# Scoring the left keys of three head pairs in one block, with their exponentials in two small tiles and the next pair's slot

## The chip, the cores and the metric

One core of one Trainium2 chip runs the whole program. The metric is the time of one execution on the device in microseconds (us); lower is better. Three runs of the kernel before gave 596.84, 598.58 and 599.66 us, a median of 598.58 us.

## The reference

Attention with RMS-normalised queries and keys over 8 batches of 12 heads, 448 tokens and 64 numbers a head, then a two-layer MLP with a residual on the 768 columns of each token.

```python
q_n, k_n = rmsnorm(q, g_q), rmsnorm(k, g_k)          # (8, 12, 448, 64)
scores = q_n @ k_n.T / 8                             # per head, 448 x 448
attn = softmax(scores) @ v
x = attn.transpose(0, 2, 1, 3).reshape(8, 448, 768)
xn = (x - mean(x)) / sqrt(var(x) + 1e-6) * g_ln
out = x + relu(xn @ w_ch1) @ w_ch2                   # 768 -> 3072 -> 768
```

## The kernel before

**Pairs, units, left keys.** The 96 heads are worked on as 48 pairs, p = 0 to 47, six to a batch. From pair 6 on two pairs make a unit, the piece in which q, k and v are loaded and normalised. A pair's keys are 2 heads x 448 tokens: three tiles of 128 keys for each head (i = 0 to 5), and a seventh tile, i = 6, that holds the last 64 keys of both heads. These last 64 are the "left" keys here. A score of i < 6 is one matmul of 128 columns of weights over 448 queries into a bank of PSUM (L388). The left score is two matmuls of 64 columns of weights each, one for a head, that write the lower and the upper 64 partitions of one bank (L394). From unit 5 on (`TWO_LEFT`) both pairs of a unit have their left scores made together, four matmuls in a row, at the first pair's i = 6; the second pair has none at that place.

**Scores, exponentials, values.** `scores` calls `score` (the matmuls) and `power` (L409: ScalarE takes the exponential of the bank into the fp16 tile `E`). `values` multiplies the exponentials by v one pair later (L446 and L448, banks oA and oB), and `evac_o` moves the sums out with VectorE. An even pair's tile has seven slots, an odd pair's six, and the odd pair's left exponentials go to a small tile `EL`.

**Banks.** Score banks are the two `psS` buffers, and, for pairs after 14, the bank `tr` as a third: `score_bank` gives every third score to it. A score waits until the exponential that last read its bank is done: of the score three places before where three banks turn, two places before where two do. The bank `tr` also takes TensorE's transposes of keys and queries (`trans_k`, `trans_q`, copied out by VectorE in `copy_k`, `copy_q`), which pairs up to 13 use. From unit 8 on (pairs 14 and 15) DMA transposes on SP's queue do that: eight for a unit, `dma_k` (L292, L295) and `dma_q` (L302, L305). They write `kU` and `qU`, of which there are two each, so those of a unit wait until the scores of the unit before the last have read the same buffer.

**The order around it.** TensorE, ScalarE, GpSimd and SP run in the order in which the code is written. Up to the middle of pair 12 the table `ORDER` is that order. After it `run_rest` writes the MLP of batch b (24 chunks "up" of six matmuls into psH, each followed by a relu on ScalarE, L1023; then "down" chunks of six into psC, L1055), and after each chunk so many steps of the attention of batch b + 1 as keep pace with it, often one, sometimes two. A step is (p, i); it writes the score of pair p and the values of pair p - 1. The MLP's odd batches have four token tiles (psH 512 wide), the even ones three (384 wide). In `attention()` a unit's preparation is spread over the steps before its first pair p: squares of keys and queries on ScalarE in steps 2 and 4 of pair p - 4, a copy of the keys (L108) in its step 6, roots (L263, L264) in step 1 of pair p - 3, the DMA transposes at the start of pair p - 2. Pairs p - 4 are even ones.

The names that the change touches: `scores`, `score`, `power`, `score_bank`, `copy_q`, `value`, the tiles E7 and E6 (also used as room by the first batch), and the loop in `attention()`.

Of the kernel before, what the change touches and what calls it, by code (L numbers as in the profile page):

```python
# [9 lines left out]
FP16 = mybir.dt.float16  # L10
# [6 lines left out]
ts = bass.ts  # L17

B, H, S, D = 8, 12, 448, 64
# [5 lines left out]
PAIR_UNIT = [(u, w) for u, (_, _, m) in enumerate(UNITS) for w in range(m)]  # L25
UNIT_PAIR = [PAIR_UNIT.index((u, 0)) for u in range(len(UNITS))]
# [38 lines left out]
H0.1.3 Y.R L10v L10q Y.X0 Y.N1 H1.1.0 E12.3 Y.X1 H1.1.1 J0.1 Y.N3 m8 S12.4 Y.X2 H1.1.2 P0.1  # L65
# [55 lines left out]
class _Fast:  # L121


    def __init__(self, ctx, tc, sh, q, k, v, gs, g_ln, w1, w2, out):
        self.gs, self.g_ln = gs, g_ln
        self.tc, self.nc, self.sh = tc, tc.nc, sh
        self.q, self.k, self.v, self.w1, self.w2, self.out = q, k, v, w1, w2, out
        nc = tc.nc
        pool = lambda name, bufs, **kw: ctx.enter_context(tc.tile_pool(name=name, bufs=bufs, **kw))
        self.p_in = pool("p_in", 2)  # L130
        self.p_n = pool("p_n", 2)
        self.p_e = pool("p_e", 1)
# [28 lines left out]
        self.late, self.preps, self.n_scores, self.sums = [], {}, 0, {}  # L161

    def load_main(self, eng, n, t, b, h0, nh):

# [194 lines left out]
    def copy_q(self, p):  # L359
        qT = self.qU[PE_SET][:, p % 2].rearrange("p e s -> p (e s)")  # L360
        self.nc.vector.tensor_copy(out=qT, in_=self.tr[:, 128:128 + 2 * S])  # L361
        kT = self.kT(p)
        self.prs[p] = dict(q=qT, main=kT[:, 192:960], left=kT[:, 0:192])

    def scores(self, p, i):

        u, w = PAIR_UNIT[p]
        both = u >= TWO_LEFT and i == 6
        if both and w:
            return  # L370
        self.score(p, i)
        for d in range(2 if both else 1):
            self.power(p + d, i)

    def score(self, p, i):

        nc = self.nc
        c = self.prs[p]
        both = PAIR_UNIT[p][0] >= TWO_LEFT and i == 6
        if i == 0:  # L380
            k = 7 - p % 2
            c["E"] = self.p_e.tile([128, k, S], FP16, tag=f"E{k}", name="E")
        ps = [self.score_bank(p + d) for d in range(2 if both else 1)]
        for d, x in enumerate(ps):
            self.prs[p + d]["ps", i] = x
        if i < 6:
            h = i // 3
            nc.tensor.matmul(ps[0][:, 0:S], c["main"][:, ts(i, 128)], c["q"][:, ts(h, S)],  # L388
                             start=True, stop=True)
        elif both:  # L390
            for d, x in enumerate(ps):
                cd = self.prs[p + d]
                for e in range(2):
                    nc.tensor.matmul(x[64 * e:64 * e + 64, 0:S], cd["left"][:, 128 * e:128 * e + 64],  # L394
                                     cd["q"][:, ts(e, S)], start=True, stop=True)
        else:
            left, q = c["left"], c["q"]
            nc.tensor.matmul(ps[0][:, 0:S], left[:, 0:128], q[:, 0:S], start=True, stop=False)
            nc.tensor.matmul(ps[0][:, 0:S], left[:, 64:192], q[:, S:2 * S], start=False, stop=True)

    def power(self, p, i):

        c, u = self.prs[p], PAIR_UNIT[p][0]
        if i < 6 or p % 2 == 0:
            o = c["E"][:, i]
        else:
            o = c["EL"] = self.p_e.tile([128, S], FP16, tag="EL", name="EL")
        g = self.group(p, i)
        self.nc.scalar.activation(out=o, in_=c.pop(("ps", i))[:, 0:S], func=AFT.Exp,  # L409
                                  scale=self.units[u][3][:, g:g + 1], bias=EXP_BIAS)  # L410
# [19 lines left out]
    def value(self, p, i):  # L430
        nc = self.nc
        c = self.prs[p]
        E = c["EL"] if i == 6 and p % 2 else c["E"][:, i]
        if i == 0:
            c["oA"] = self.ps_o.tile([128, 3, 130], FP32, tag="oA", name="oA")
            c["oB"] = self.ps_o.tile([128, 130], FP32, tag="oB", name="oB")
        oA, oB = c["oA"], c["oB"]
        if i < 6:
            h, j = divmod(i, 3)
            rhs = self.v16[:, p % 6, h, j]  # L440
            cs = slice(65 * h, 65 * h + 65)
        else:
            rhs = self.vl[:, p % 6].rearrange("p e d -> p (e d)")
            cs = slice(0, 130)
        for t in range(3):
            nc.tensor.matmul(oA[:, t, cs], E[:, ts(t, 128)], rhs,  # L446
                             start=(i == 0 and t == 0), stop=(i == 6 and t == 2))
        nc.tensor.matmul(oB[:, cs], E[:, 320:448], rhs, start=(i == 0), stop=(i == 6))  # L448

# [26 lines left out]
    def first_pieces(self):  # L476
# [9 lines left out]
        E7 = self.p_e.tile([128, 7, S], FP16, tag="E7", name="E").rearrange("p k s -> p (k s)")  # L486
        E6 = self.p_e.tile([128, 6, S], FP16, tag="E6", name="E").rearrange("p k s -> p (k s)")
# [154 lines left out]

        def room(ph, p):
            if ph < 2:
                return (E7 if p < 3 else E6)[:, 896 * (p % 3):896 * (p % 3) + 896]
            return (E6 if p in (2, 3) else E7)[:, 1344 * (p % 2):1344 * (p % 2) + 1344]
# [224 lines left out]
    def attention(self):  # L871
# [25 lines left out]
        for p in range(nb0, n + 1):  # L897
            for i in range(7):
# [1 line left out]
                if i == 0 and p < n and p % NPAIR == 0 and p > nb0:  # L900
                    c.append(lambda b=p // NPAIR: self.batch(b))
                c += todo.pop(7 * p + i, [])
                if p < n and f"S{p}.{i}" not in done and i < 6:
                    c.append(lambda p=p, i=i: self.scores(p, i))
                if p > nb0:
                    for x in {0: (), 1: (0, 1)}.get(i, (i,)):
                        if f"V{p - 1}.{x}" not in done:
                            c.append(lambda p=p, x=x: self.values(p - 1, x))
                if p < n and i == 6 and f"S{p}.6" not in done:
                    c.append(lambda p=p: self.scores(p, 6))  # L910
                if p > nb0 + 1 and i == 1 and (p - 1) % NPAIR and p > 2 * NPAIR:
                    c.append(lambda p=p: self.stats(p - 2))
                if p + 1 < UNIT_PAIR[DMA_UNIT]:
# [419 lines left out]
```

## Time and profile before

| what | us |
|---|---|
| median of three runs | 598.58 (596.84 to 599.66) |
| the profiled execution, its own time | 597.09 |
| its span, first to last instruction | 595.4 |
| VectorE, ScalarE, GpSimd busy | 290.0, 350.9, 191.5 |
| "up" stages of batches 1 to 6 begin at | 112.94, 192.69, 254.28, 330.93, 392.53, 469.18 |
| the "down" stages after them begin at | 154.63, 225.66, 293.80, 363.90, 432.05, 502.15 |
| granted TensorE clock | 0.999 of full speed |

The profile gives the busy time of each engine (PE is TensorE's matmuls, PEld its weight loads, DVE VectorE, ACT ScalarE, POOL GpSimd, SPq the queue that issues DMAs on SP), groups of instructions by line, and for each idle stretch of an engine what ended it. In the timeline a row gives the start and the length of one or several merged instructions. Matmuls overlap: the length of a row is from a matmul's start to the end of its pipeline, and what it costs is the distance to the next one's start.

### The profile page before, as it was taken

The page shows a single profiled execution, that of the slowest core. Times are in us where ns is not written, and L with a number is a line of the kernel's source. Part 1 is how long each engine was busy: PE and PEld are TensorE (multiplying, and loading weights), DVE is VectorE, ACT ScalarE, POOL GpSimd, SP SyncE. Part 2 cuts the span into 40 slices and gives each one's busy share as a digit, 9 for nine tenths or more (in the row PEclk, how much of TensorE's full clock was granted, in tenths as well). Part 3 has the DMA queues.
Part 4 walks back from the last instruction along what each step waited for, and adds up shares of the span by engine and source line. Part 5 has one row for each costly group of instructions (what it writes and reads, how often), then busy time and mean ns, then how long its engine had stood idle before and what let it go on. Part 6 is the DMA issues. An engine that isn't in the chain of part 4 may idle for free.

```text
span 595.4 us, 12406 instructions
## 1 busy us (share of the span) xinstructions
PE 580.2 (97%) x4973; PEld 360.0 (60%) x4973; DVE 290.0 (49%) x634; ACT 350.9 (59%) x664; POOL 191.5 (32%) x256
## 2 busy tenths in 40 slices
PE   5899999999999999999999999999999999999997
PEld 4688986544565666655566666654566666654565
DVE  6999787244455256724356255724256322440011
ACT  6898684279751897358843598538755377114300
POOL 4568550044550555133541345423412000000000
PEclk9999999999999999999999999999999999999999
DMA  8999999725985686945955587849633320040011
GB/s 262 208 243 236 221 233 198 181 72 98 155 157 132 134 152 111 191 117 65 153 139 117 94 138 153 171 122 126 127 66 88 86 63 1 28 106 1 1 53 56
DMA packets 130225, 75.24 MB, mean 126 GB/s; under 512 B 96469, under 2 KB 120357, under 8 KB 130165
## 3 DMA queue, kind: packets, MB, share of 16 engines
q1 hardware_dynamic: 113712, 44.94, 38.3%
q0 software_dynamic: 16128, 29.27, 23.1%
q8 instruction: 40, 0.66, 0.5%
q10 hardware_dynamic: 324, 0.21, 0.1%
q14 instruction: 21, 0.16, 0.1%
HBM read 52.30 MB, written 11.01 MB: 106 GB/s over the span
## 4 chain that ended last, share of the span: by engine, by line
PE 91%; DVE 3%; ACT 2%; DMA 2%; issue 1%; SPq 1%; ACTq 0%
PE psC L1055 36%; PE psH L1021 32%; PE psS L388 8%; PE oA L446 5%; PE psU L718 4%; PE oB L448 2%; PE psS L394 1%; DMA hT<-in_k_dram 1%; SPq L166 1%; PE psS L662 1%; PE tr L339 1%; DMA xnT<-xn 1%; DVE qn L581 0%; ACT khl L116 0%; PE tr L356 0%
## 5 line engine op out<-in xcount | busy, mean ns | idle before, releaser
L1055 PE MATMUL psC<-w,hT 128*128 128x384 f16 (+1 forms) x1368 | 235.5, 323 | 0.0
L1021 PE MATMUL psH<-xnT,w 128*128 128x512 f16 (+1 forms) x1008 | 217.8, 356 | 0.1
L409 ACT ACTIVATE E<-psS,rr_all 128x448 f16<-128x448 f32 x273 | 171.1, 636 | 61.9 <-PE psS L388 61.0
L1055 PEld LDWEIGHTS <-hT 128*128 128x128 f16 x1368 | 127.3, 98 | 78.7 <-issue 3.9
L1023 ACT ACTIVATE hT<-psH 128x512 f16<-128x512 f32 (+1 forms) x168 | 93.7, 558 | 121.4 <-PE psH L1021 120.2
L1021 PEld LDWEIGHTS <-w 128*128 128x128 f16 x1008 | 91.0, 98 | 78.0 <-issue 3.0
L388 PE MATMUL psS<-qU,kU 128*128 128x448 f16 x252 | 86.5, 352 | 0.7 <-ACT E L409 0.6
L446 PEld LDWEIGHTS <-E 128*128 128x128 f16 x819 | 56.1, 98 | 35.3 <-issue 1.4
L268 POOL TENSOR_TENSOR qkv<-qkv,gprod 128x896 f32<-128x896 f32 x20 | 41.6, 2079 | 86.1 <-ACT khl L116 66.0
L1062 DVE SCALAR_TENSOR_TENSOR x<-psC,rs_all,x 128x384 f32<-128x384 f32 x48 | 29.2, 616 | 80.7 <-PE psC L1055 80.2
L446 PE MATMUL oA<-v,E 128*128 128x65 f16 x756 | 58.0, 193 | 0.1
L166 POOL DMA_DIRECT2D qkv<-in_k_dram x14 | 11.2, 797 | 122.8 <-ACT E L409 68.2
L459 DVE RECIPROCAL rec_all<-oA 128x6 f32<-128x6 f32 x42 | 8.2, 195 | 86.4 <-PE oA L446 86.1
L448 PE MATMUL oB<-v,E 128*128 128x65 f16 x252 | 45.2, 193 | 0.1
L260 DVE TENSOR_REDUCE ssq<-khl 128x14 f32<-128x896 f32 x21 | 22.7, 1083 | 45.6 <-ACT khl L116 45.5
L388 PEld LDWEIGHTS <-kU 128*128 128x128 f16 x252 | 24.3, 98 | 16.8 <-DVE qU L361 0.2
L260 DVE TENSOR_REDUCE ssq<-qn 128x14 f32<-128x896 f32 x21 | 22.8, 1085 | 22.2 <-ACT qn L116 21.0
L91 DVE SCALAR_TENSOR_TENSOR qn<-qkv,rr_all 128x256 f16<-128x256 f32 (+2 forms) x71 | 25.3, 416 | 16.9 <-ACT rr_all L264 16.9
L718 PE MATMUL psU<-xnT,w 128*128 128x128 f16 x432 | 26.9, 219 | 0.0
L448 PEld LDWEIGHTS <-E 128*128 128x128 f16 x273 | 26.3, 96 | 0.2 <-DVE xl L466 0.2
L718 PEld LDWEIGHTS <-w 128*128 128x128 f16 x432 | 25.1, 98 | 1.4 <-issue 0.5
L461 DVE TENSOR_TENSOR x<-oA,rec_all 128x384 f32<-128x384 f32 x42 | 23.4, 558 | 1.3
(158 smaller groups left out, 591.9 us busy)
## 6 DMA issues: line engine op xcount, KB each, us to landing
out_dram<-x SPq DMA_DIRECT2D x20, 384.0 KB, 2.6
qkv<-in_v_dram POOLq DMA_DIRECT2D x15, 384.0 KB, 7.3
qkv<-in_k_dram POOLq DMA_DIRECT2D x14, 384.0 KB, 3.8
qkv<-in_q_dram POOLq DMA_DIRECT2D x14, 384.0 KB, 5.3
w<-in_moe_w_ch_dram POOLq DMA_DIRECT2D x3, 1536.0 KB, 12.8
w<-in_moe_w_ch_dram POOLq DMA_DIRECT2D x2, 2304.0 KB, 22.8
qkv<-in_q_dram SPq DMA_DIRECT2D x7, 384.0 KB, 8.8
qkv<-in_v_dram SPq DMA_DIRECT2D x6, 384.0 KB, 13.1
```

The lines of the kernel that those rows point to most:

```text
L91: nc.vector.scalar_tensor_tensor(out=out, in0=x, scalar=8.0, in1=r.unsqueeze(2).broadcast_to([x.shape[0], g, D]), op0=ALU.mult, op1=ALU.mult)
L260: nc.vector.tensor_reduce(out=c["ssq"][:, n], in_=c["sq", n], axis=AX.X, op=ALU.add)
L268: _on(nc, f"i{u}", "P").tensor_tensor(out=self.loads[u][1], in0=self.loads[u][1], in1=sh.gprod.unsqueeze(1).broadcast_to([128, g, D]), op= ...
L388: nc.tensor.matmul(ps[0][:, 0:S], c["main"][:, ts(i, 128)], c["q"][:, ts(h, S)], start=True, stop=True)
L409: self.nc.scalar.activation(out=o, in_=c.pop(("ps", i))[:, 0:S], func=AFT.Exp, scale=self.units[u][3][:, g:g + 1], bias=EXP_BIAS)
L446: nc.tensor.matmul(oA[:, t, cs], E[:, ts(t, 128)], rhs, start=(i == 0 and t == 0), stop=(i == 6 and t == 2))
L448: nc.tensor.matmul(oB[:, cs], E[:, 320:448], rhs, start=(i == 0), stop=(i == 6))
L718: nc.tensor.matmul(ps[:, ts(f, 128)], sh.w1[:, dc, ts(4 * k + f, 128)], self.xnT[:, dc, ts(t, 128)], start=(f == 0 and dc == 0), stop=(f = ...
L1021: nc.tensor.matmul(ps[:, 0:N], sh.w1[:, dc, ts(f, 128)], xnT[:, dc, 0:N], start=(dc == 0), stop=(dc == NDC - 1))
L1023: nc.scalar.activation(out=hT[:, f, 0:N], in_=ps[:, 0:N], func=AFT.Relu)
L1055: nc.tensor.matmul(self.psC[:, 0:g[1]], self.hT[:, f, ts(t, 128)], sh.w2[:, h, f, c:c + g[1]], start=(f == 0), stop=(f == NFF - 1))
L1062: self.nc.vector.scalar_tensor_tensor(out=x, in0=self.sums.pop((b, t, g[0]))[:, 0:g[1]], scalar=self.rs[:, b, t:t + 1], in1=x, op0=ALU.mul ...
```

## The change

From pair 12 on the left scores of three pairs 3m, 3m + 1 and 3m + 2 are made in one block of six matmuls. In a batch's six pairs the two blocks stand in pair 1 after its score 3 (with scores 4 and 5 behind it, one step later than before), and in pair 3 at its place 6. Pairs 0, 2 and 5 have no left score at their place 6, and pair 4's score 5 comes one step later. All pairs' tiles have six slots now. The exponentials of pair 3m's left keys go to slot 5 of the next pair's tile, which that pair fills later; the other two go to two `EL` buffers. Pair 13's TensorE transposes and copies (K13, C13, Q13, D13) stand in the table, and the bank `tr` is a third score bank as soon as the last of them is written.

```diff
-Y.X3 H1.1.3 J1.1 H2.1.0 H2.1.1 J2.0 S12.5 P1.1 P2.0 y8 H2.1.2 H2.1.3 E12.5 J2.1 P2.1 E12.4 M
+H0.1.3 Y.R L10v L10q Y.X0 Y.N1 H1.1.0 E12.3 Y.X1 H1.1.1 J0.1 Y.N3 m8 S12.4 K13 C13 Y.X2 H1.1.2
+P0.1 Y.X3 H1.1.3 J1.1 H2.1.0 H2.1.1 J2.0 S12.5 Q13 D13 P1.1 P2.0 y8 H2.1.2 H2.1.3 E12.5 J2.1
+P2.1 E12.4 M
...
+THREE_LEFT = 12
...
     def copy_q(self, p):
...
+        self.all_turned = p + 1 == UNIT_PAIR[DMA_UNIT]
...
     def scores(self, p, i):
-        u, w = PAIR_UNIT[p]
-        both = u >= TWO_LEFT and i == 6
-        if both and w:
+        if i == 6:
+            self.left_scores(self.left_pairs(p))
             return
         self.score(p, i)
-        for d in range(2 if both else 1):
-            self.power(p + d, i)
+        self.power(p, i)
+
+    def score_at(self, p, i):
+        if p < THREE_LEFT or p % 6 == 3:
+            return i
+        return {1: (0, 1, 2, 3, 6, 4, 5), 4: (0, 1, 2, 3, 4, None, 5)}.get(
+            p % 6, (0, 1, 2, 3, 4, 5, None))[i]
+
+    def left_pairs(self, p):
+        if p >= THREE_LEFT:
+            return range(p - p % 3, p - p % 3 + 3)
+        if PAIR_UNIT[p][0] >= TWO_LEFT:
+            return () if PAIR_UNIT[p][1] else (p, p + 1)
+        return (p,)
+
+    def left_scores(self, pairs):
+        for x in pairs:
+            self.left_score(x)
+        for x in pairs:
+            self.power(x, 6)
...
+    def open_powers(self, p):
+        c = self.prs[p]
+        if "E" not in c:
+            c["E"] = self.p_e.tile([128, 6, S], FP16, tag=f"E{p % 2}", name="E")
+
+    def left_score(self, p):
         nc = self.nc
         c = self.prs[p]
-        both = PAIR_UNIT[p][0] >= TWO_LEFT and i == 6
...
+        for e in range(2):
+            nc.tensor.matmul(ps[64 * e:64 * e + 64, 0:S], left[:, 128 * e:128 * e + 64],
+                             q[:, ts(e, S)], start=True, stop=True)
...
     def power(self, p, i):
         c, u = self.prs[p], PAIR_UNIT[p][0]
-        if i < 6 or p % 2 == 0:
             o = c["E"][:, i]
+        elif p >= THREE_LEFT and p % 3 == 0:
+            self.open_powers(p + 1)
+            o = c["EL"] = self.prs[p + 1]["E"][:, 5]
         else:
-            o = c["EL"] = self.p_e.tile([128, S], FP16, tag="EL", name="EL")
+            o = c["EL"] = self.p_e.tile([128, S], FP16, tag="EL", name="EL", bufs=2)
...
     def score_bank(self, p):
         self.n_scores += 1
-        if p > UNIT_PAIR[DMA_UNIT] and self.n_scores % 3 == 2:
+        if self.all_turned and self.n_scores % 3 == 2:
...
-                if p < n and f"S{p}.{i}" not in done and i < 6:
-                    c.append(lambda p=p, i=i: self.scores(p, i))
+                at = self.score_at(p, i)
+                score = lambda p=p, at=at: self.scores(p, at)
+                go = p < n and at is not None and f"S{p}.{at}" not in done
+                if go and i < 6:
+                    c.append(score)
...
-                if p < n and i == 6 and f"S{p}.6" not in done:
-                    c.append(lambda p=p: self.scores(p, 6))
+                if go and i == 6:
+                    c.append(score)
```

How the instructions move is seen in three places. The first is TensorE in the first "up" stage of the attention of batch 2, at the left scores of pair 14 (before, with pair 15) and of pairs 15, 16 and 17 (after). The rows are from the program before. In a row, the line comes first, then the operation, the tile written and the tiles read; psS is a score bank, kU0 or kU1 the unit's turned keys; a row that stands for the second head's matmul reads like the first and is left out.

```order
L448 MATMUL oB_2509<-vl_109,EL_2359 128x130
L394 LDWEIGHTS kU0_104
L394 MATMUL psS_2598<-qU0_106,kU0_104 64x448
...
L394 MATMUL psS_2599<-qU0_106,kU0_104 64x448
L1021 LDWEIGHTS w1_68
L1021 MATMUL psH_2608<-xnT_2191,w1_68 128x512
```

The same place in the changed program, three pairs of it, and what follows.

```order
L475 MATMUL oB_2626<-vl_109,EL_2432 128x130
L422 LDWEIGHTS kU0_104
L422 MATMUL psS_2714<-qU0_106,kU0_104 64x448
...
L422 LDWEIGHTS kU1_105
L422 MATMUL psS3_2717<-qU1_107,kU1_105 64x448
...
L422 MATMUL psS_2720<-qU1_107,kU1_105 64x448
L404 LDWEIGHTS kU1_105
L404 MATMUL psS_2743<-qU1_107,kU1_105 128x448
L1051 LDWEIGHTS w1_68
L1051 MATMUL psH_2746<-xnT_2194,w1_68 128x512
```

The block takes all three banks (psS3 is `tr`), reads two units' keys, and here has pair 16's first score behind it with no MLP chunk between. Of the twelve blocks one is followed by a score at once, three by four value matmuls and then a score, the other eight by a chunk of the MLP before the next score.

The second place is ScalarE beside these blocks; before, then after. L1023 (L1053 after the change) is the relu of a chunk, L409 (L436) the exponential, L108 the copy of a unit's keys.

```order
L409 ACTIVATE E_2488<-psS_2574,rr_all_1828 128x448
L1023 ACTIVATE hT_120<-psH_2581 128x512
L108 ACTIVATE khl_2531<-qkv_2063 128x14x64
L409 ACTIVATE E_2488<-psS_2598,rr_all_1828 128x448
L409 ACTIVATE EL_2606<-psS_2599,rr_all_1828 128x448
L1023 ACTIVATE hT_120<-psH_2608 128x512
```

```order
L436 ACTIVATE E_2607<-psS_2689,rr_all_1830 128x448
L1053 ACTIVATE hT_120<-psH_2696 128x512
L436 ACTIVATE E_2723<-psS_2714,rr_all_1830 128x448
L436 ACTIVATE EL_2725<-psS3_2717,rr_all_2331 128x448
L436 ACTIVATE EL_2728<-psS_2720,rr_all_2331 128x448
L436 ACTIVATE E_2723<-psS_2743,rr_all_2331 128x448
L1053 ACTIVATE hT_120<-psH_2746 128x512
```

The block has left the even pair's place 6, where the copy of the keys stands ahead of its exponentials; it has three exponentials in a row, the first into the tile (E_2723) that the next score's exponential writes too.

The third place is TensorE at pair 13's transposes into `tr`, at the end of the table. Before, keys and queries followed each other within the "up" stage of batch 1:

```order
L1021 MATMUL psH_2302<-xnT_2191,w1_68 128x512
L336 LDWEIGHTS khl_1525
L336 MATMUL tr_121<-id16_58,khl_1525 128x2x64
...
L339 MATMUL tr_121<-id16_58,khl_1525 128x128
L353 LDWEIGHTS qn_1524
L353 MATMUL tr_121<-id16_58,qn_1524 128x2x64
...
L1021 MATMUL psH_2326<-xnT_2191,w1_68 128x512
```

After the change the keys' stand behind pair 12's score 4 and the queries' behind its score 5, in the "down" stage of batch 0:

```order
L404 MATMUL psS_2217<-qU1_107,kU1_105 128x448
L339 LDWEIGHTS khl_1526
L339 MATMUL tr_121<-id16_58,khl_1526 128x2x64
...
L1085 MATMUL psC_2198<-w2_62,hT_120 128x384
...
L404 MATMUL psS_2257<-qU1_107,kU1_105 128x448
L356 LDWEIGHTS qn_1525
L356 MATMUL tr_121<-id16_58,qn_1525 128x2x64
...
L1085 MATMUL psC_2243<-w2_62,hT_120 128x384
```

24 matmuls of the MLP now lie between the keys' transposes and the queries'.

More of the change, by code (lines that the diff above doesn't have):

```diff
@@ L161, in __init__ @@
         self.late, self.preps, self.n_scores, self.sums = [], {}, 0, {}
+        self.all_turned = False
     def load_main(self, eng, n, t, b, h0, nh):
@@ new lines, in left_pairs @@
+    def left_pairs(self, p):
[9 more added lines that the diff above has]
+            self.power(x, 6)
+    def score(self, p, i):
+        if i == 6:
+            for x in self.left_pairs(p):
+                self.left_score(x)
+            return
+        c = self.prs[p]
+        if i == 0:
+            self.open_powers(p)
+        c["ps", i] = ps = self.score_bank(p)
+        self.nc.tensor.matmul(ps[:, 0:S], c["main"][:, ts(i, 128)], c["q"][:, ts(i // 3, S)],
+                              start=True, stop=True)
@@ L377, in score @@
+    def open_powers(self, p):
+        c = self.prs[p]
+        if "E" not in c:
+            c["E"] = self.p_e.tile([128, 6, S], FP16, tag=f"E{p % 2}", name="E")
+    def left_score(self, p):
         nc = self.nc
         c = self.prs[p]
-        both = PAIR_UNIT[p][0] >= TWO_LEFT and i == 6
[L380 to L399, printed above, removed]
+        c["ps", 6] = ps = self.score_bank(p)
@@ L401, in power @@
+        left, q = c["left"], c["q"]
+        if PAIR_UNIT[p][0] < TWO_LEFT:
+            nc.tensor.matmul(ps[:, 0:S], left[:, 0:128], q[:, 0:S], start=True, stop=False)
+            nc.tensor.matmul(ps[:, 0:S], left[:, 64:192], q[:, S:2 * S], start=False, stop=True)
+            return
+        for e in range(2):
+            nc.tensor.matmul(ps[64 * e:64 * e + 64, 0:S], left[:, 128 * e:128 * e + 64],
+                             q[:, ts(e, S)], start=True, stop=True)
     def power(self, p, i):
@@ L432, in value @@
         c = self.prs[p]
-        E = c["EL"] if i == 6 and p % 2 else c["E"][:, i]
+        E = c["EL"] if i == 6 else c["E"][:, i]
         if i == 0:
@@ L485, in first_pieces @@
         wide = [x.rearrange("p w e s -> p (w e s)") for x in self.qU]
[L486 to L487 removed]
+        Ea = self.p_e.tile([128, 6, S], FP16, tag="E0", name="E").rearrange("p k s -> p (k s)")
+        Eb = self.p_e.tile([128, 6, S], FP16, tag="E1", name="E").rearrange("p k s -> p (k s)")
         self.batch(0)
@@ L644, in room @@
             if ph < 2:
-                return (E7 if p < 3 else E6)[:, 896 * (p % 3):896 * (p % 3) + 896]
-            return (E6 if p in (2, 3) else E7)[:, 1344 * (p % 2):1344 * (p % 2) + 1344]
+                return (Ea if p < 3 else Eb)[:, 896 * (p % 3):896 * (p % 3) + 896]
+            return (Eb if p in (2, 3) else Ea)[:, 1344 * (p % 2):1344 * (p % 2) + 1344]
         PARTS = {2: (((0, 0, 192), (1, 0, 192), (2, 0, 128)), ((2, 128, 192), (3, 0, 192), (4, 0, 192)),
```

2 lines of the change are left out of this document (1 added, 1 removed).

## The prediction, on record before the run

> **What bounds the kernel now.** I read the page first, then the stages, the waits, and the timeline around one block. From the page of the profile:
>
> ```profile
> span 595.4 us, 12406 instructions
> ...
> PE 580.2 (97%) x4973; PEld 360.0 (60%) x4973; DVE 290.0 (49%) x634; ACT 350.9 (59%) x664; POOL 191.5 (32%) x256
> ...
> PE 91%; DVE 3%; ACT 2%; DMA 2%; issue 1%; SPq 1%; ACTq 0%
> ```
>
> TensorE is busy 97% of the span and 91% of the chain that ended last, so a change pays here only by matmul time saved or by idle time of TensorE; all of that is 595.4 - 580.2 = 15.2 us. The view by stretches, for the "up" stages of batches 1, 2 and 4 (span, then the busy time of each engine, then the granted clock and the share of the DMA engines):
>
> ```profile
> 113.00:154.00 41.00, 39.93 (x269) 19.75 (x270) 16.64 (x38) 30.64 (x56) 18.77 (x26) 1.00 0.48 104
> 192.70:225.70 33.00, 33.00 (x290) 20.57 (x289) 14.91 (x37) 28.87 (x60) 18.52 (x26) 1.00 0.76 138
> 330.90:363.90 33.00, 33.00 (x290) 20.54 (x288) 14.87 (x37) 28.83 (x60) 18.42 (x26) 1.00 0.86 136
> ```
>
> TensorE is full there at the full clock, but ScalarE has 28.8 of 33 us to do, so a burst on it finds little slack. The waits of TensorE from 112 us on, and where the left scores are seen as a group:
>
> ```profile
> PE tr L353 <- DVE kU L346: 0.8, 1, 0.8
> PE psS L388 <- ACT E L409: 0.6, 3, 0.2
> ...
> L394 PE MATMUL psS<-qU,kU x80: 352/365/377, 71.4 to 501.9; 128*64 128x448 f16 x80
> ```
>
> So where the change works (all of the 80/4 = 20 blocks of left scores but the first two, which the table holds) TensorE loses 1.4 us in waits. Nothing of 3 us (0.5%, about what a measurement of this kernel can tell from no change) can be gained there beyond the matmuls' own cost.
>
> **The blocks: 18 of two pairs become 12 of three.** One block of two, in time order, and the same values followed by a chunk without a block (338.82, 338.87); the row at 347.12 is the second pair's two matmuls, from a view that cuts into the block:
>
> ```profile
> 338.82 0.22 PE L448 MATMUL oB<-vl,E 128*128 128x130 f16 x1
> 338.87 1.14 PE L1021 MATMUL psH<-xnT,w 128*128 128x384 f16 x6
> ...
> 346.59 0.33 PE L446 MATMUL oA<-vl,EL 128*128 128x130 f16 x3
> 346.76 0.22 PE L448 MATMUL oB<-vl,EL 128*128 128x130 f16 x1
> 346.91 0.57 PE L394 MATMUL psS<-qU,kU 128*64 128x448 f16 x4
> ...
> 347.12 0.35 PE L394 MATMUL psS<-qU,kU 128*64 128x448 f16 x2
> ...
> 347.41 1.15 PE L1021 MATMUL psH<-xnT,w 128*128 128x384 f16 x6
> ```
>
> From the value matmul to the chunk it is 0.65 us with the block and 0.05 without: a block of two costs 0.60. Its pairs start 0.21 apart, less than half of that, so 0.60 - 2 x 0.21 = 0.18 is paid for going in and out. A block of three then costs 0.81, and six pairs 2 x 0.81 = 1.62 instead of 3 x 0.60 = 1.80. Six batches: **-1.1 us**. Bounds: if the third pair cost as much as half a block (0.30), nothing; if it started as close as an ordinary score's 0.19, -1.3. I take the row's 0.21.
>
> [...]
>
> **Pair 13's transposes.** They move from the "up" stage into the "down" stage before it. Their matmuls cost the same there; the wait between them does not move along. The first two rows are from the new place, pair 12's score 4 and the 24 matmuls behind it, the others from the old one:
>
> ```profile
> 106.49 0.35 PE L388 MATMUL psS<-qU,kU 128*128 128x448 f16 x1
> 106.68 4.06 PE L1055 MATMUL psC<-w,hT 128*128 128x384 f16 x24
> ...
> 118.72 0.66 DVE L346 COPY kU<-tr 128x960 f16<-128x960 f16 x1 [4.87 <-PE tr L339]
> 119.43 0.22 PE L353 MATMUL tr<-id,qn 128*128 128x128 f16 x1 [0.75 <-DVE kU L346]
> ```
>
> The queries' transposes waited 0.75 us for VectorE's 0.66 us copy out of `tr`. At the new place 4.06 us of matmuls cover that copy, six times its length; without that cover the 0.75 would be back. **-0.75 us**, bounds -0.75 and 0.
>
> **Waits for a bank that go.** Three scores waited for an exponential:
>
> ```profile
> 124.65 0.35 PE L388 MATMUL psS<-qU,kU 128*128 128x448 f16 x1 [0.18 <-ACT E L409]
> ...
> 227.18 0.35 PE L388 MATMUL psS<-qU,kU 128*128 128x448 f16 x1 [0.19 <-ACT E L409]
> ...
> 365.43 0.35 PE L388 MATMUL psS<-qU,kU 128*128 128x448 f16 x1 [0.18 <-ACT E L409]
> ```
>
> The first is pair 13's, with two banks in turn; it now has three. The other two are the second of two scores behind a block whose exponentials stood behind the copy of the keys; the block has left that place. **-0.55 us**; at least nothing, at most the 0.6 of the list.
>
> **Waits for a bank that come.** A block of three takes every bank. The next score needs the bank of the block's first pair, and the block's third pair the bank of the score just before the block. What ScalarE does around the block above:
>
> ```profile
> 346.61 0.51 ACT L1023 ACTIVATE hT<-psH 128x384 f16<-128x384 f32 x1
> ...
> 346.98 0.67 ACT L409 ACTIVATE E<-psS,rr_all 128x448 f16<-128x448 f32 x1
> ...
> 347.50 0.53 ACT L1023 ACTIVATE hT<-psH 128x384 f16<-128x384 f32 x1
> 347.87 1.00 ACT L108 ACTIVATE khl<-qkv 128x896 f16<-128x896 f32 x1
> 348.39 0.35 PE L388 MATMUL psS<-qU,kU 128*128 128x448 f16 x1
> ...
> 348.71 0.68 ACT L409 ACTIVATE E<-psS,rr_all 128x448 f16<-128x448 f32 x1
> 349.22 0.69 ACT L409 ACTIVATE EL<-psS,rr_all 128x448 f16<-128x448 f32 x1
> ```
>
> An exponential holds ScalarE 0.51 (348.71 to 349.22) and is done after 0.68; a relu of 384 holds it 0.37 and starts 0.02 after its chunk. In the new places (odd pairs, places 4 and 6) there is no copy of keys. With the block's start as zero, its first pair ends at 0.38 (0.57 less 0.21, and a little), the last chunk's relu is over by then, so the first exponential runs from about 0.4 to 1.05. A score directly behind the block would start at 0.29 + 2 x 0.21 = 0.72 and waits about 0.35 (one place); with four value matmuls between, which are half as wide as the four from 346.59 to 346.81 and so take some 0.13, it waits 0.2 (three places); with a chunk of 1 us between, not at all (eight). The third pair starts at 0.43: where a chunk lies between it and the score before, that score's exponential is long done; only the last batch's second block has none between, up to 0.3. Sum 0.35 + 3 x 0.2 + 0.2 = 1.15; an exponential late by half its length at these places (ScalarE is 87% busy) adds some. **+1.4 us**, bounds 0.6 and 2.5 (0.5 each at five places). Queued behind a late score are only the next chunk's matmuls, so the loss is the wait itself.
>
> **Transposes that are needed earlier.** The block in pair 3 reads pair 4's and 5's keys and queries, and pair 1's last score, which frees their buffer, comes a step later. Where slack is least, unit 18 (pairs 34, 35):
>
> ```profile
> 337.36 0.35 PE L388 MATMUL psS<-qU,kU 128*128 128x448 f16 x1
> ...
> 337.75 2.27 SPq L292 DMA_TRANSPOSE kU<-khl  x1
> 340.07 5.37 SPq L295 DMA_TRANSPOSE kU<-khl  x2
> ...
> 349.44 3.56 SPq L305 DMA_TRANSPOSE qU<-qn  x2
> ...
> DMA to landing us min/median/max: 4.2/4.2/4.2
> ...
> 355.31 0.22 PE L448 MATMUL oB<-vl,E 128*128 128x130 f16 x1
> ```
>
> They start when pair 31's score 5 (337.36) ends. Of the last two the first landed 4.2 after its start, at 353.6 (the row of landings, from the view of L305); the second was issued at 353.0, and for its landing I take 354.1, an estimate. Now pair 31's score 5 stands a chunk and some values later, by about 2.3 us, so the last lands at about 356.4, and the block stands behind the values at 355.31, say at 355.9 with the other shifts, its second pair at 356.1. They meet within 0.3 us. For unit 12, in a batch of the same kind, the same sum leaves 2 us:
>
> ```profile
> 199.50 2.48 SPq L292 DMA_TRANSPOSE kU<-khl  x1
> ...
> 208.58 3.72 SPq L305 DMA_TRANSPOSE qU<-qn  x2
> ...
> 216.90 0.33 PE L446 MATMUL oA<-vl,E 128*128 128x130 f16 x3
> ```
>
> (issued by 212.3, landed by 213.4, + 2.3 = 215.7, needed at about 217.7.) Batches with 512-wide chunks have longer steps and more slack. **+0.3 us**, bounds 0 and 4.3 (rival B). The block in pair 1 reads pair 2's transposes, which start with pair 0; pair 0's steps run ahead of the last 13 chunks (of 1 us each) of the batch before, so these have time.
>
> **Semaphores inside a block.** The first reader of a unit's transposes has extra wait instructions:
>
> ```profile
> L388 PEldq EVENT_SEMAPHORE  x32: 51/51/51, 130.9 to 492.7; - x32
> ```
>
> Before they stood ahead of a 128-wide score under a running chunk. Ten or so units are now first read inside a block, between short matmuls. Two of 51 ns for each of 12 blocks would be 1.2 us; hidden, nothing. **+0.3 us**.
>
> Sum: -1.1 - 0.75 - 0.55 + 1.4 + 0.3 + 0.3 = **-0.4 us**. The profiled execution took 597.09, so it would take 596.7 with a span of 595.0; the median of the runs is 1.49 higher, and against it the forecast is **598.1 us**.
>
> **The rivals.** *A: none of the new waits binds.* The exponential of the block's first pair is always in time, the transposes too, and the semaphores are hidden: the +2.0 goes, -2.4 is left, 596.2 us. For it speaks that ScalarE's heavy pieces stand in even pairs, and the blocks now in odd ones; against it the arithmetic at the score directly behind a block.
>
> *B: the transposes come late.* The place is the second pair of the block in pair 3 of batches 3, 5 and 7, and it decides once eight transposes take over 16 us from pair 1's last score. Unit 18 took 15.3 us to issue, with 5.4 for its two L295 while the DMA engines were 0.86 busy; unit 12 took 12.8. With another 3 us of such sticking in the two batches that still load, unit 18 is late by 3.3 and unit 12 by 1: +4.3 instead of +0.3, 602.1 us. Against it: in the list above TensorE waits for no DMA at all.
>
> *C: ScalarE falls behind in every block.* Three exponentials in a row hold it 1.5 us, and relus behind them free psH late. If each of the 12 blocks cost TensorE 0.5, the +1.4 becomes 6.0: 602.7 us. It decides from a backlog over one chunk; against it, 4 us of slack in each 33.
>
> *D: a third pair drains like a block of its own.* Nothing is saved on the blocks: +0.7 in sum, 599.3 us.
>
> **How the numbers follow.** The forecast 0.47, A 0.18, B 0.12, C 0.11, D 0.12. The forecast's own range is 596.5 to 600, which covers A and D nearly; B and C, 0.23 together, reach over 601.6, so the upper end must go to 601.7 to leave out no more than about half of them, and the lower to 595.5 for A with a run-to-run spread like the one shown (596.84 to 599.66). Faster by over 0.5% (under 595.6) 0.13: A at its bounds. Slower by over 0.5% (over 601.6) 0.19: B and most of C. Same 0.68.
>
> **What would show it.** After the change the left matmuls start in threes 0.21 apart, 14 blocks in all; no wait of queries' transposes at 119 us; waits of scores for exponentials of 0.2 to 0.4 at four or five places, all right behind blocks. A wait for a DMA on a left score, above all near 356 us, would be B; waits of psH for relus C. I am wrong if TensorE's idle time after 113 us grows or shrinks by over 2 us.

## The result, and the profile after

The changed kernel took 595.89 us (median of 10 runs, 594.75 to 598.48) against 598.66 before (10 runs, 596.84 to 599.66): a ratio of 0.9962, 95% interval 0.9949 to 0.9975, so 0.38% faster. The forecast was 598.1, faster by 0.1%.

The profiled execution happens to be the slowest of its ten. Its page and its list of TensorE's waits from 40 us on (what waited for what: total, times, longest):

```profile
span 596.8 us, 12425 instructions
...
PE 578.8 (97%) x4973; PEld 360.6 (60%) x4973; DVE 289.0 (48%) x634; ACT 352.0 (59%) x664; POOL 192.9 (32%) x256
...
PE psS L404 <- ACT EL L436: 2.2, 2, 2.0
...
PE psS L404 <- ACT E L436: 1.0, 4, 0.4
```

The span is longer than before's 595.4, although TensorE is busy 1.4 us less. The wait of 2.0 us stands in the table's part, and neither of the two other profiles of the same kernel has it:

```profile
93.42 0.35 PE L404 MATMUL psS<-qU,kU 128*128 128x448 f16 x1 [2.01 <-ACT EL L436]
```

So total spans of single executions can't be compared here: the part ahead of the first "up" chunk of batch 1, where the loads of the first inputs run, differs by up to 3 us from one execution of this kernel to another. The stretch from that chunk to the end is steady, and the readings below rest on it. The second profile of the changed kernel, page and the row of the chunk:

```profile
span 593.9 us, 12425 instructions
...
PE 579.4 (98%) x4973; PEld 361.7 (61%) x4973; DVE 289.2 (49%) x634; ACT 351.6 (59%) x664; POOL 193.5 (33%) x256
```

```profile
113.93 1.24 PE L1051 MATMUL psH<-xnT,w 128*128 128x512 f16 x5
```

593.9 - 113.9 = 479.9; in the three profiles of the changed kernel it is 479.93, 479.92 and 480.16, in two of the kernel before 482.50 and 482.73. Of these 2.6 us, 0.8 is work that moved ahead of the stretch (pair 13's transposes), as this view of the second profile shows at their new place:

```profile
106.92 0.35 PE L404 MATMUL psS<-qU,kU 128*128 128x448 f16 x1
107.11 0.22 PE L339 MATMUL tr<-id,khl 128*128 128x128 f16 x1
107.17 0.50 PE L342 MATMUL tr<-id,khl 128*128 128x128 f16 x6
107.50 4.06 PE L1085 MATMUL psC<-w,hT 128*128 128x384 f16 x24
```

Seven transposes cost 107.50 - 107.11 = 0.39 us, the two sets 0.78; no wait is left. So the change gains 1.8 us in the stretch.

A block of three, from the timeline of the second profile, whole and then cut after its second and its first pair:

```profile
354.10 0.22 PE L475 MATMUL oB<-vl,EL 128*128 128x130 f16 x1
354.25 0.76 PE L422 MATMUL psS<-qU,kU 128*64 128x448 f16 x6
354.94 0.50 PE L1051 MATMUL psH<-xnT,w 128*128 128x384 f16 x2
```

```profile
354.25 0.57 PE L422 MATMUL psS<-qU,kU 128*64 128x448 f16 x4
```

```profile
354.25 0.38 PE L422 MATMUL psS<-qU,kU 128*64 128x448 f16 x2
```

From the value matmul to the chunk it is 0.84 us, 0.05 of it without a block: a block of three costs 0.79 where a block of two cost 0.60. Two blocks of three in place of three blocks of two save 1.80 - 1.58 = 0.22 in each batch, 1.3 in six. The third pair adds 0.19, as an ordinary score does, not 0.21; the starts in the trace are 0, 213 and 403 ns.

A score behind a block with four value matmuls between, in the second profile (TensorE, then ScalarE):

```profile
197.61 0.76 PE L422 MATMUL psS<-qU,kU 128*64 128x448 f16 x6
198.30 0.27 PE L473 MATMUL oA<-v,E 128*128 128x65 f16 x3
198.41 0.19 PE L475 MATMUL oB<-v,E 128*128 128x65 f16 x1
198.78 0.35 PE L404 MATMUL psS<-qU,kU 128*128 128x448 f16 x1 [0.19 <-ACT E L436]
...
199.06 0.19 PE L475 MATMUL oB<-v,E 128*128 128x65 f16 x1
199.09 0.32 PE L1051 MATMUL psH<-xnT,w 128*128 128x384 f16 x1
```

```profile
197.72 0.49 ACT L1053 ACTIVATE hT<-psH 128x384 f16<-128x384 f32 x1 [0.27 <-PE psH L1051]
198.11 0.63 ACT L436 ACTIVATE E<-psS,rr_all 128x448 f16<-128x448 f32 x1
198.62 1.16 ACT L436 ACTIVATE EL<-psS,rr_all 128x448 f16<-128x448 f32 x2
```

The first exponential runs from 0.50 to 1.13 us after the block's start and the score begins 0.04 later. The idle time in the score's brackets is 0.19, but the instruction behind that value matmul normally starts 0.03 later (199.06, 199.09) and here starts 0.37 later: the score lost 0.34, because idle time is counted only from the modelled end of the matmul before (198.41 + 0.19 = 198.60). Read so, from start to start against the same pair of instructions elsewhere in the trace, the five waits behind and in blocks cost 0.46, 0.44, 0.35, 0.35 and 0.24, together 1.84 us.

### The profile page after: what moved, and what is told of

The parts are those of the page before. It is cut to its first block, busy times and chain, and to the rows that moved or that the text cites. A ratio compares the mean times of both kernels' runs of the same rounds, so it can differ in the third digit from the quotient of the medians.

```text
span 596.8 us, 12425 instructions
## 1 busy us (share of the span) xinstructions
PE 578.8 (97%) x4973; PEld 360.6 (60%) x4973; DVE 289.0 (48%) x634; ACT 352.0 (59%) x664; POOL 192.9 (32%) x256
## 4 chain that ended last, share of the span: by engine, by line
PE 82%; DMA 9%; SPq 3%; POOL 2%; ACT 1%; issue 1%; DVE 1%; POOLq 0%; DVEq 0%
PE psC L1085 36%; PE psH L1051 33%; PE psS L404 7%; PE oA L473 4%; DMA qkv<-in_v_dram 4%; DMA qkv<-in_k_dram 2%; DMA qkv<-in_q_dram 2%; SPq L169 2%; PE oB L475 2%; SPq L177 1%; PE psS L422 1%; DMA w<-in_k_dram 1%; ACT E L436 0%; ACT hT L1053 0%; POOL qkv L271 0%
## 5 line engine op out<-in xcount | busy, mean ns | idle before, releaser
L436 ACT ACTIVATE E<-psS,rr_all 128x448 f16<-128x448 f32 x264 | 165.1, 635 | 62.6 <-PE psS L404 62.3
L1053 ACT ACTIVATE hT<-psH 128x512 f16<-128x512 f32 (+1 forms) x168 | 93.6, 557 | 110.5 <-PE psH L1051 108.9
L473 PEld LDWEIGHTS <-E 128*128 128x128 f16 x792 | 53.7, 98 | 35.4 <-issue 3.1
L475 PEld LDWEIGHTS <-E 128*128 128x128 f16 x264 | 25.4, 96 | 0.3 <-DVE xl L493 0.2
```

Of the source, the lines that this page charges most:

```text
L473: nc.tensor.matmul(oA[:, t, cs], E[:, ts(t, 128)], rhs, start=(i == 0 and t == 0), stop=(i == 6 and t == 2))
L1053: nc.scalar.activation(out=hT[:, f, 0:N], in_=ps[:, 0:N], func=AFT.Relu)
```

## The experiments

The stretch from the first "up" chunk of batch 1 to the end, in each profile. The third column adds 0.8 where pair 13's transposes stand ahead of the stretch, so that it can be compared down the column.

| kernel | stretch, us | same work | median, runs | ratio to before |
|---|---|---|---|---|
| before (two profiles) | 482.50, 482.73 | 482.6 | | 0.9989 (0.9975 to 1.0004) |
| changed (three profiles) | 479.93, 479.92, 480.16 | 480.8 | 595.89, 595.67, 595.93 | 0.9962, 0.9958, 0.9955 |
| e1 list only | 480.28 | 481.1 | 596.09 | 0.9962 (0.9948 to 0.9977) |
| e2 blocks only | 480.95 | 480.9 | 596.66 | 0.9972 (0.9958 to 0.9986) |
| e4 chunk apart (two profiles) | 478.17, 478.33 | 479.0 | 594.34, 594.41 | 0.9929, 0.9925 |
| e5 blocks of one | 482.88 | 483.7 | one run | |
| e7 tiles only | 481.69 | 481.7 | 596.98 | 0.9979 (0.9967 to 0.9991) |
| e8 transposes late | 490.16 | 491.0 | one run | |
| e9, e10 twice | 499.18, 503.21 | 500.0, 503.2 | one run each | |

**One part alone.** e1 has blocks of two, e2 the old place of pair 13's transposes, e7 both, so only the tiles and the earlier third bank are left in it. The table's rows are cut to the entries that differ.

```diff
-THREE_LEFT = 12            # e1, e7
+THREE_LEFT = 99
-m8 S12.4 K13 C13 Y.X2      # e2, e7
+m8 S12.4 Y.X2
-J2.0 S12.5 Q13 D13 P1.1
+J2.0 S12.5 P1.1
```

> The changed kernel with blocks of two as before (the bound from which three pairs are scored together set past the last pair); kept are pair 13's transposes in the table, the third bank from pair 13 on, tiles of six slots and two small tiles. Theory (the gain is the sum of the parts seen after 113 us in the two traces): the 0.75 us wait of the queries' transposes goes and the first waits for a bank shrink, so 0.8 to 1.2 us faster than before, about 0.15 to 0.2%. Rival (the gain comes from the tiles and the order in the table, ahead of 113 us): 2 us or more faster, as much as the whole change.

> The changed kernel with pair 13's transposes back in the steps of pair 12, behind the table; blocks of three stay. Theory: blocks of three at 0.79 instead of 0.81 us save 1.3 us, new waits behind blocks cost about as much as the old bank waits that go, and the 0.75 us wait between keys' and queries' transposes is back: 0.8 to 1.5 us faster than before, 0.15 to 0.25%. Rival (the parts need each other: the third bank comes too late for the first block): no gain, and a wait of over 0.5 us at the first block.

> The changed kernel with blocks of two and pair 13's transposes back in the steps of pair 12: what is left of the change is the tiles (six slots for all, two small ones), and the third bank from the end of pair 13's transposes on. Theory (the list's transposes are what the kernel with blocks of two gains by): within 0.15% of before, about 0.5 us faster by the earlier third bank, and the 0.75 us wait between the transposes is back. Rival (the tiles give the early part more room): 1.5 us or more faster, nearly as much as with the transposes in the table.

In the stretch, e7 gains 0.8 to 0.9 over before, e1 1.5, e2 1.7, the change 1.8. e7's share is larger than the expected 0.5: the three waits for a bank that the earlier third bank removes (before at 124.65, 128.35 and 138.81 us) lose 0.34, 0.17 and 0.29 us from start to start, 0.8 together, of which the list of idle times shows only the first. The last of them in the kernel before:

```profile
138.49 0.19 PE L448 MATMUL oB<-v,E 128*128 128x65 f16 x1
138.81 0.35 PE L388 MATMUL psS<-qU,kU 128*128 128x448 f16 x1
```

Putting the transposes into the table adds 0.6 to that (e7 to e1). Blocks of three add 0.3 on top (e1 to the change), since most of what the matmuls save goes to the new waits. e2 stands only 0.1 behind the change: it pays 0.9 more for the transposes at their old place, but it has four waits in and behind blocks (0.34, 0.35, 0.35 and 0.23) where the change has five, 0.6 less. Its profile also has waits of 0.9 for a copy and 0.7 for a DMA, both ahead of the stretch.

By medians the parts look larger: e1 is 1.85 us under the kernel before and e7 1.55, above what both expectations said, and for e7 within its rival's "1.5 us or more", a gain in the early part. The traces don't bear that rival out: e7's first "up" chunk came at 112.83 us, hardly earlier than before's 112.94 and 113.31, and the kernel before, run again beside e7 (e6 below), stood 0.9 under the same reference runs. The intervals, 0.3% wide, can't separate the parts.

**The change and the kernel before, again.**

> The changed kernel as it is, beside the others on the same chip. Theory: the parts add, 1.6 to 2.5 us faster than before. Its second profile should show no 2 us wait near 93 us if that wait was a chance of one execution, and the same wait if the two small tiles cause it.

> The kernel before, as it is. It shows how far the stretch ahead of the first up chunk (112.94 us in its first profile; 113.9 to 117.8 in the changed kernel and the three others) varies between executions, and that the stretch after it does not. Theory: 482.5 us again from the first up chunk to the end, within 0.5, and a first up chunk somewhere between 113 and 117. Rival: the changed kernel is quicker ahead of that chunk, and 112.94 was a lucky execution: 115 or later here.

> The changed kernel as it is, a third time. Theory: 479.9 us from the first up chunk to the end, and 1.6 to 2.3 us under the kernel before.

The stretches repeat within 0.25 us. By medians the change is 2.3 us faster than before in e3, as expected, and 2.8 in e12, more than the 1.6 to 2.3 expected there. The first "up" chunk came at 116.91, 113.93 and 114.38 us in the changed kernel and at 112.94 and 113.31 before; with 0.8 of moved work in the former no gain ahead of it is seen. The 2 us wait at 93 us did not come back: it was a chance of one execution. The kernel before, submitted beside its own reference runs, came out at 597.65 against 598.53, ratio 0.9989, with an interval that takes in 1. So some of the 2.3 to 2.8 us in the comparisons of medians may not be the change's; against that 597.65, which was not run beside them, the change's medians are 1.7 to 2.0 lower, as the stretch says. Where the remaining 0.5 to 1 us lies is open.

**A chunk on both sides of every block (e4, e11).** A step that holds a block is written alone.

```diff
+        self.blocks = set()
...
+                if go and at == 6:
+                    self.blocks.add(len(steps))
                 if c:
                     steps.append(c)
...
     def upto(self, target):
+        ran = False
         while self.pos < min(target, len(self.steps)):
+            block = self.pos in self.blocks
+            if block and ran:
+                break
             for call in self.steps[self.pos]:
                 call()
             self.pos += 1
+            ran = True
+            if block:
+                break
```

> The changed kernel, with one rule more where steps are written behind the MLP's chunks: a step that holds a block is written alone, so a chunk stands between the score before it, the block, and the score behind it. Theory (a score behind a block waits for the block's first exponential only because no chunk is between): the waits of 0.2 to 0.4 us behind four blocks and inside the last block go, 1.3 us of idle time, 1.2 to 1.8 us faster than the changed kernel. Rival (ScalarE's backlog sets them): the waits move to the next scores, less than 0.5 us gained.

> The kernel with a chunk on both sides of every block, again, beside the changed kernel on the same chip. Theory: from the first up chunk to the end 478.2 us again, and 1.7 us under the changed kernel's median. Rival (its first comparison was helped by the chip): less than 0.8 us under it.

478.2 and 478.3 instead of 479.9: 1.7 us, the 1.84 of the five waits nearly whole. The ratio to before is 0.9929 (0.9913 to 0.9945) and 0.9925 (0.9909 to 0.9941), and beside the changed kernel the median is 1.3 and 1.5 us lower. From 100 us on TensorE's list of waits is empty. The place of the wait above, in e4's timeline:

```profile
197.72 0.76 PE L423 MATMUL psS<-qU,kU 128*64 128x448 f16 x6
198.41 0.27 PE L474 MATMUL oA<-v,E 128*128 128x65 f16 x3
198.52 0.19 PE L476 MATMUL oB<-v,E 128*128 128x65 f16 x1
198.54 1.14 PE L1054 MATMUL psH<-xnT,w 128*128 128x384 f16 x6
199.52 0.35 PE L405 MATMUL psS<-qU,kU 128*128 128x448 f16 x1
```

The chunk starts 0.02 after the value matmul, and the score, 1.80 after the block's start, finds its bank free. So the waits came from the lack of a chunk, not from ScalarE's backlog: they did not move to the next scores. In both comparisons this version is ahead of the changed kernel too, by 0.2% of its time.

**What a block pays for being one (e5).** Every pair's left score stands alone at its own place 6.

```diff
     def score_at(self, p, i):
-        if p < THREE_LEFT or p % 6 == 3:
-            return i
+        return i
...
         if p >= THREE_LEFT:
-            return range(p - p % 3, p - p % 3 + 3)
+            return (p,)
...
-        elif p >= THREE_LEFT and p % 3 == 0:
-            self.open_powers(p + 1)
-            o = c["EL"] = self.prs[p + 1]["E"][:, 5]
```

> The changed kernel with each pair's left score alone at its own place 6 from pair 12 on: 36 blocks of one instead of 12 of three. Theory (each block pays once for going into and out of the half-width matmuls, about 0.18 to 0.2 us, and 0.2 a pair): a block of one costs 0.39 us, 36 of them 14.0 us against 9.5 for 12 of three, so 4 us and a little more in the stretch from the first up chunk to the end (479.9 in the changed kernel, then 483 to 485; less the bank waits of about 1.3 that go). Rival D (each pair drains for itself, nothing hangs on the number of blocks): the stretch shrinks by the bank waits alone, to 478.5.

A block of one in its timeline:

```profile
307.20 0.22 PE L471 MATMUL oB<-vl,EL 128*128 128x130 f16 x1
307.35 0.38 PE L421 MATMUL psS<-qU,kU 128*64 128x448 f16 x2
307.66 1.15 PE L1081 MATMUL psC<-w,hT 128*128 128x384 f16 x6
```

It costs 0.46 - 0.05 = 0.41, so 36 of them 14.8 us against 9.5 for 12 of three: 5.3 more, less the 1.84 of waits that it doesn't have, 3.4. Measured 483.7 - 480.8 = 2.9, in one execution, and 482.88 is just under the expected 483 to 485; the other 0.5 is not explained. Rival D (478.5) is out: one, two and three pairs cost 0.41, 0.60 and 0.79, that is 0.22 a block and 0.19 a pair.

**Transposes late.** e8 moves the DMA transposes of units 9 to 24 four steps later in the written order; e9 (the changed kernel) and e10 (the one before) issue the key transposes of units 12, 18 and 24 twice.

```diff
-                at = st + (e - st) * x // (k - 1) if x < k else e + 1 + x - k
+                at = st + (e - st) * x // (k - 1) if x < k else e + 1 + x - k + (4 if u > DMA_UNIT else 0)
```

```diff
         def dma_k():
+            for _ in range(2 if u in (12, 18, 24) else 1):
+                keys()
+
+        def keys():
```

> The changed kernel with the DMA transposes of all units after the first (units 9 to 24) issued four steps later, some 5 us. It measures the margin of rival B. By the landing times in the changed kernel's trace, 2.5 to 3.5 us are left at units 12, 18 and 24: late by about 2 us in each of three batches, 4 to 8 us more in the stretch from the first up chunk, with TensorE waiting for transposes at the block in pair 3. If nothing is lost, the margin is wider than the landings say.

It lost 10.2 us, more than the expected 4 to 8, and not at a block. Unit 12's transposes started at 200.59 us as before (200.68): on SP's queue nothing that waits longer came ahead of them (the issue before them, at 192.16, was over by 193.27), and they start when the scores that free their buffer are done: in the first profile of the changed kernel the transposes of each of units 9 to 24 start 0.03 to 0.04 us after a score ends, unit 12's at 203.66 after one that ends at 203.63. The loss is at the "up" stages of batches 3 and 5. TensorE's waits, and its row at the first of them:

```profile
PE psH L1051 <- DMA xnT<-xn: 6.9, 2, 3.6
...
256.14 2.72 PE L1051 MATMUL psH<-xnT,w 128*128 128x512 f16 x6 [3.29 <-DMA xnT<-xn]
```

SP's queue there in e8, and in the second profile of the changed kernel:

```profile
246.65 2.51 SPq L308 DMA_TRANSPOSE qU<-qn  x2
249.26 5.23 SPq L1033 DMA_TRANSPOSE xnT<-xn  x4
```

```profile
241.56 2.53 SPq L308 DMA_TRANSPOSE qU<-qn  x2
...
244.82 5.29 SPq L1033 DMA_TRANSPOSE xnT<-xn  x4
```

The batch's own transposes (xnT) stand behind unit 14's on the same queue and were 4.4 us later with them. So this experiment says nothing on the margin at the blocks.

> The changed kernel with the key transposes of units 12, 18 and 24 (the second units of the three-tile batches) issued twice, the second time with the same data: three more DMA transposes ahead of each of these units' queries, about 5 us of SP's queue. By the trace of the changed kernel its second run, 2.5 to 3.4 us are left between the last landing and the block's second pair there. Theory (the change cut the margin, rival B has its point there): late by 1.5 to 2.5 us at each, so the stretch from the first up chunk grows from 479.9 to 484 to 488, with the waits on the left scores of pairs 22, 34 and 46. Rival (the margin is wider): under 481.

> The kernel before with the same three units' key transposes issued twice. There the keys and the first head's queries are needed only at pair 22's, 34's and 46's own first score, 2.7 to 6 us after the last landing in its trace. Theory: late by 2 us at unit 18 at most, the stretch from the first up chunk grows from 482.5 to 483 to 485, less than half of what the changed kernel loses. Rival (the change cut no margin): both kernels lose the same.

Both expectations were too small: at unit 12 the second writing began 3.5 us after the issue of the first had ended in e9 (208.68, then 212.21) and 3.8 in e10 (205.31, then 209.14), by inference because it waited for the first to land, and at units 12 and 18 the queries' transposes were issued 5 to 9 us later, not 5. The waits on transposes, e9 and then e10:

```profile
PE psS L425 <- DMA qU<-qn: 11.3, 4, 6.7
...
226.56 0.55 PE L425 MATMUL psS<-qU,kU 128*64 128x448 f16 x1 [6.74 <-DMA qU<-qn]
227.91 0.91 PE L425 MATMUL psS<-qU,kU 128*64 128x448 f16 x3 [0.80 <-DMA qU<-qn]
```

```profile
PE psS L391 <- DMA qU<-qn: 16.2, 2, 11.3
...
223.75 0.53 PE L391 MATMUL psS<-qU,kU 128*128 128x448 f16 x1 [4.83 <-DMA qU<-qn]
```

At unit 12 the changed kernel waits 7.5 us, inside the block, where the one before waits 4.8 at pair 22's first score. At unit 24 it is 0.45 against nothing. At unit 18 the kernel before lost more, 11.3 against 6.7, and in total both lost about 20 us (19.3 and 20.6), as e10's rival said.

The order at unit 18 comes from the transposes, not from the margin. On SP's queue 7.9 us lie between the first key transposes' end and the second ones in e10, and 2.1 in e9, as these rows of e10 and then of e9 show:

```profile
348.07 2.99 SPq L298 DMA_TRANSPOSE kU<-khl  x2
358.94 1.27 SPq L295 DMA_TRANSPOSE kU<-khl  x1
```

```profile
353.46 2.52 SPq L301 DMA_TRANSPOSE kU<-khl  x2
358.11 1.28 SPq L298 DMA_TRANSPOSE kU<-khl  x1
```

The margin can be read without doubling anything, from the start of unit 18's transposes to the first matmul that needs the queries. In the kernel before that is pair 34's first score, in its first profile at 356.34, and the transposes began at 337.75:

```profile
356.34 0.35 PE L388 MATMUL psS<-qU,kU 128*128 128x448 f16 x1
```

In the second profile of the changed kernel it is the block's second pair, at 354.46, and the transposes began at 338.46:

```profile
338.46 3.04 SPq L295 DMA_TRANSPOSE kU<-khl  x1
...
348.04 2.52 SPq L308 DMA_TRANSPOSE qU<-qn  x2
```

So the transposes have 16.0 us where they had 18.6, and at unit 12 it is 16.0 and 18.6 again. The change cuts the margin by 2.6 us. That it makes the kernel as a whole more sensitive to late transposes these two executions do not show.

## Why the prediction was right, and what it got wrong

The direction was right, and so was the change being under 0.5%. The signs that the prediction named came too: left matmuls in threes in 14 blocks, no wait of the queries' transposes, waits at five places behind or in blocks, none for a DMA and none of psH for a relu. The size was not right: the sum was -0.4 us, and 1.8 came in the stretch. The measured 595.89 lies only 0.4 above the lower end of the range, which had been set for rival A, and 0.3 from A's 596.2. That closeness to A is luck: A needed that no new wait binds, and they cost 1.84 us. (By the prediction's own sum, 598.58 - 0.4, the forecast is 598.2, not 598.1.) Term by term, against the stretch's 1.8 us:

| term of the sum | forecast | from start to start in the traces |
|---|---|---|
| 12 blocks of three for 18 of two | -1.1 | -1.3 |
| pair 13's transposes | -0.75 | -0.9 (1.69 at the old place, 0.78 at the new) |
| bank waits that go | -0.55 | -1.5 |
| bank waits that come | +1.4 | +1.84 |
| transposes late | +0.3 | 0 |
| semaphores in a block | +0.3 | 0 |
| sum | -0.4 | -1.9, measured -1.8 |

- **Blocks.** Right, near its bound of -1.3: the third pair starts 0.19 behind the second (403 - 213 = 190 ns), as an ordinary score does, where 0.21 had been reckoned; from the first pair to the second it is 213 ns.
- **Bank waits that go.** This is the term that was mis-sized most. It was taken from idle times (0.18, 0.19, 0.18), which count from the modelled end of the matmul before. From start to start the same places lose 0.34, 0.35 and 0.35, and two more, at 128.35 and 138.81, that were left out lose 0.17 and 0.29: 1.5 in sum. The new waits had been worked out from start to start, so the two terms were not in the same measure, and the loss weighed more than the gain.
- **Bank waits that come.** Mechanism and places were right: four scores behind blocks and the third pair of the last block, 0.24 to 0.46 each where 0.2 to 0.35 was reckoned. In the block shown above the first exponential started 0.50 us after the block, not 0.4; e4 removes these waits and gets 1.7 us.
- **Late transposes.** The distance was right: the prediction had the transposes start at 337.75 + 2.3 and the block's second pair at 356.1, that is 16.05 us, and the trace has 16.0. What was off is the time of the transposes themselves. To issue unit 18's took 15.3 us in the profile that the estimate was read from and 15.0 in the other one of the kernel before, but 12.1, 11.4 and 11.4 in the three of the changed kernel; why is not shown. In the second profile the last was issued at 349.3, and its neighbour took 2.9 to land:

```profile
DMA to landing us min/median/max: 2.9/2.9/2.9
```

  By that the last landed at about 352.2, an estimate, 2.2 us ahead of the pair that needs it.
- **Semaphores.** Blocks that read a unit's transposes first have the same starts, 0, 213 and 403 ns, as those that don't: hidden. Rival A's condition held for these two terms, and failed for the banks.
- Rival C is out (waits at 5 places, not 12, and none of psH for a relu), and D by e5. B was not met; e9 and e10 show what it would take.

## What to carry to other kernels

Where TensorE is full, count a wait from the start of the instruction before to the start of the waiting one, against the same pair of instructions elsewhere in the trace; idle time understates it (0.19 for a loss of 0.34 behind the block at 197.61). When work that takes several buffers at once is grouped, put other work on both sides of the group: here the rule gained 1.7 us, nearly as much as the whole change before it. And a transfer that is needed earlier must be looked at together with what stands behind it on its queue: in e8 the batch's own transposes came 4.4 us later.

## What was not expected of the hardware

After TensorE had been idle 3.3 us (e8), its matmuls ran at half speed for 2.9 us, at a granted clock of 0.50. The last chunk ahead of that stretch, and the view by stretches of e8 while TensorE was idle, at half speed and behind it (the column ahead of the last two is the granted clock):

```profile
251.71 1.14 PE L1085 MATMUL psC<-w,hT 128*128 128x384 f16 x6
```

```profile
252.90:255.50 2.60, 0.00 (x0) 0.00 (x0) 0.60 (x1) 0.00 (x0) 0.00 (x0) 1.00 0.78 151
255.60:258.90 3.30, 2.76 (x7) 1.02 (x8) 0.00 (x0) 0.00 (x1) 0.00 (x0) 0.50 0.68 242
259.00:262.00 3.00, 3.00 (x22) 1.52 (x21) 0.50 (x2) 2.48 (x6) 0.00 (x0) 1.00 0.02 4
```

Seven matmuls were granted half the clock, 259.00 - 256.14 = 2.86 us for what takes 1.48 in the changed kernel: 1.4 us more than the wait, and 1.6 at the other place. Of e8's 10.2 us, 7.3 are the two waits, counted from start to start (6.9 by idle time), and 2.9 are this. The granted clock was still 1.00 up to 255.5 and had fallen by 255.6, when TensorE had been idle 2.7 us (251.71 + 1.14 = 252.85); it was back 2.9 us after the first matmul. No run here shows what sets these two times.
